# The loads of q, k and v issued from GpSimd instead of SyncE, in a retention layer followed by two feed-forward blocks

## The chip, the cores and the metric

One core of a Trainium2 chip. The metric is the time of one execution on the device in microseconds (us). The engines are TensorE (PE in the profile; its weight loads are PEld), VectorE (DVE), ScalarE (ACT), GpSimd (POOL) and SyncE (SP), which here does nothing but issue transfers. Transfers run on 16 DMA engines, which all issuers share.

## The reference

Three layers run one after the other. The first is a linear attention with decay: for each of 4 batches and 8 heads a 64x64 state is decayed and updated with each of 768 tokens.

```
state = gamma * state + outer(k[t], v[t])
y[t]  = scale * q[t] @ state                  # B=4, H=8, S=768, D=64
```

Its 3072 x 512 result goes through a gated block and then through a block with a sigmoid gate:

```
x = ((x @ w1) * (x @ w2)) @ w3 @ w_out        # 512 -> 1024 -> 1024 -> 512
h = x @ w_in                                  # 512 -> 2048
out = (h * sigmoid(1.702 * h)) @ w_out2       # 2048 -> 512
```

The weights are handed over as 64-bit numbers, and the kernel converts them itself.

## The kernel before

The attention is done in 24 chunks of 128 tokens, six for each batch, in chunked form: scores of a chunk (k by q), a causal mask with decay, outputs from the masked scores and from the state, and an update of the state. All q, k and v values of one chunk are packed into one array of 128 partitions x 2048 floats, 1 MB, so that one transfer fetches them; only the first chunk is fetched in two halves. `Attention.load(c)` (line 203) does that, into one of four buffers named `qkv`. What comes out of a chunk is scaled into `xb` (L291) and stored to device memory (`xd`, L295), except for the first four chunks, which stay on the chip.

The order of the work is written out by hand and is the program order of every engine's queue. `Attention.run` goes over the chunks: in iteration c come the scores of chunk c+1 (L223), the mask (L235), the state update (L249, copied to `state` by ScalarE in L263), `load(c + 3)`, and the outputs of chunk c (L270 from the masked scores, L280 from the state; the first chunk of a batch has no L280). The load of chunk c+3 takes the buffer of chunk c-1, whose last reader is the outputs of chunk c-1.

Between these parts `fill` puts steps of the weight conversion. One weight tile is two halves of 512 columns and ten steps, most of them on VectorE (L112, L104, L121, L125, L133), with ScalarE in L95 and L99. Raw weights come in transfers of 0.5 MB (`fetch`, L85) into five buffers named `raw`; a buffer is free again when L133 has read it, and the next fetch is issued at that point of the program. Every transfer goes through SyncE's queue, in program order: a fetch that waits for VectorE holds whatever stands behind it.

When enough weights are converted, `fill` also multiplies `w3` by `w_out` on TensorE (`psw`, L162 to L164), two half products for each chunk; this is called the mixing here. Then follow the gated block and the last block in tiles of 512 tokens, in which TensorE has matmuls without a break. All of their products are made of three matmuls of split numbers (`mm3`, L162 to L164).

Ahead of the loop the kernel issues, in this order, the load of chunk 0, the mask, the decay factors `dv`, two fetches, the loads of chunks 1 and 2 with factors between them, and three more fetches; two memsets on GpSimd (L336) clear the state.

Of the kernel before, what the change touches and what calls it, by code (L numbers as in the profile page):

```python
# [37 lines left out]
def tile_kernel(  # L38
# [13 lines left out]
    nc = tc.nc  # L52
# [133 lines left out]
    class Attention:  # L186
# [16 lines left out]
        def load(self, c):  # L203
            t = self.tile("qkv", 2048, 4)
            for h in ((0, 1024), (1024, 2048)) if c == 0 else ((0, 2048),):
                nc.sync.dma_start(t[:, slice(*h)], qkv[c][:, slice(*h)])
            qkt[c] = t[:, :1024].rearrange("p (a n t) -> p a n t", a=2, n=NP)
            kvt[c] = t[:, 1024:].rearrange("p (a h d) -> p a h d", a=2, h=H)

# [405 lines left out]
```

## Time and profile before

| | us |
|---|---|
| median of 3 runs | 1090.16 (1087.97 to 1090.22) |
| the profiled execution | 1093.12 |
| its span, from the first instruction to the last | 1091.3 |
| TensorE busy in it | 1056.6 |
| VectorE busy | 485.2 |
| ScalarE busy | 320.6 |
| GpSimd busy | 1.2 |
| bytes moved by the DMA engines | 94.80 MB |

All durations of the trace come from one execution, so sums are made against its 1093.12 us, 1.8 us of which lie around the span. Busy times of engines overlap and don't add up to the span. An issue of a transfer is short on the queue that issues it; the transfer itself goes on for microseconds after.

### The profile page before, as it was taken

The page shows a single profiled execution, that of the slowest core. Times are in us where ns is not written, and L with a number is a line of the kernel's source. Part 1 is how long each engine was busy: PE and PEld are TensorE (multiplying, and loading weights), DVE is VectorE, ACT ScalarE, POOL GpSimd, SP SyncE. Part 2 cuts the span into 40 slices and gives each one's busy share as a digit, 9 for nine tenths or more (in the row PEclk, how much of TensorE's full clock was granted, in tenths as well). Part 3 has the DMA queues.
Part 4 walks back from the last instruction along what each step waited for, and adds up shares of the span by engine and source line. Part 5 has one row for each costly group of instructions (what it writes and reads, how often), then busy time and mean ns, then how long its engine had stood idle before and what let it go on. Part 6 is the DMA issues. An engine that isn't in the chain of part 4 may idle for free.

```text
span 1091.3 us, 13274 instructions
## 1 busy us (share of the span) xinstructions
PE 1056.6 (97%) x5472; PEld 878.1 (80%) x5472; DVE 485.2 (44%) x824; ACT 320.6 (29%) x554; POOL 1.2 (0%) x6
## 2 busy tenths in 40 slices
PE   5779999999999999999999999999999999999998
PEld 4668887888888888888888888888888888888887
DVE  4778888841222221565567752232233233223222
ACT  2233334431212211333344432222222222223222
POOL 0000000000000000000000000000000000000000
PEclk9789999999999999999999999999999999999999
DMA  9888855511010100433323201001001001001001
GB/s 350 288 298 274 290 184 183 182 53 55 10 59 20 58 14 6 135 97 127 105 75 119 77 20 59 1 20 59 1 19 58 1 20 58 1 11 49 1 1 39
DMA packets 38989, 94.80 MB, mean 87 GB/s; under 512 B 3600, under 2 KB 13968, under 8 KB 35984
## 3 DMA queue, kind: packets, MB, share of 16 engines
q1 hardware_dynamic: 38928, 93.95, 25.4%
q8 instruction: 43, 0.70, 0.3%
q14 instruction: 18, 0.15, 0.0%
HBM read 76.11 MB, written 17.83 MB: 86 GB/s over the span
## 4 chain that ended last, share of the span: by engine, by line
PE 92%; DMA 3%; DVE 3%; ACT 1%; issue 1%; SPq 0%
PE psm L164 16%; PE psm L162 16%; PE psm L163 16%; PE acc L164 12%; PE acc L162 12%; PE acc L163 12%; DMA qkv<-in_qkv_dram 3%; PE s L223 2%; PE psw L164 1%; PE psw L162 1%; PE psw L163 1%; PE y L270 1%; PE y L280 1%; DVE pt L235 1%; PE u L249 1%
## 5 line engine op out<-in xcount | busy, mean ns | idle before, releaser
L164 PE MATMUL psm<-xh,wl 128*128 128x512 f32 x768 | 298.9, 389 | 1.5 <-DVE wl L104 1.5
L162 PE MATMUL psm<-xh,wh 128*128 128x512 f32 x768 | 298.8, 389 | 0.0
L163 PE MATMUL psm<-xl,wh 128*128 128x512 f32 x768 | 298.8, 389 | 0.0
L491 DVE TENSOR_TENSOR tmp<-tmp,psm 128x512 f32<-128x512 f32 x96 | 65.9, 687 | 260.7 <-ACT tmp L490 260.7
L164 PEld LDWEIGHTS psm<-xh,wl 128*128 128x128 f32 x768 | 144.2, 188 | 31.9 <-DVE wl L104 2.0
L163 PEld LDWEIGHTS psm<-xl,wh 128*128 128x128 f32 x768 | 144.2, 188 | 30.0
L162 PEld LDWEIGHTS psm<-xh,wh 128*128 128x128 f32 x768 | 144.1, 188 | 29.6
L164 PE MATMUL acc<-wh,hl 128*128 128x512 f32 x384 | 149.4, 389 | 0.0
L163 PE MATMUL acc<-wl,hh 128*128 128x512 f32 x384 | 149.4, 389 | 0.0
L162 PE MATMUL acc<-wh,hh 128*128 128x512 f32 x384 | 149.4, 389 | 0.0
L411 ACT CAST hh<-tmp 128x512 fp32r<-128x512 f32 x144 | 89.4, 621 | 198.2 <-DVE tmp L430 124.0
L412 DVE TENSOR_TENSOR hl<-tmp,hh 128x512 fp32r<-128x512 f32 x144 | 99.6, 692 | 98.9 <-ACT hh L411 98.9
L490 ACT ACTIVATE tmp<-psm 128x512 f32<-128x512 f32 x96 | 57.3, 597 | 280.4 <-PE psm L164 279.5
L430 DVE TENSOR_TENSOR tmp<-tmp,psm 128x512 f32<-128x512 f32 x48 | 33.0, 688 | 184.3 <-PE psm L164 177.0
L162 PEld LDWEIGHTS acc<-wh,hh 128*128 128x128 f32 x384 | 72.1, 188 | 15.0
L164 PEld LDWEIGHTS acc<-wh,hl 128*128 128x128 f32 x384 | 72.0, 188 | 15.1
L163 PEld LDWEIGHTS acc<-wl,hh 128*128 128x128 f32 x384 | 72.1, 188 | 14.9
L162 PE MATMUL acc<-hh,wh 128*128 128x512 f32 x192 | 74.7, 389 | 0.0
L163 PE MATMUL acc<-hl,wh 128*128 128x512 f32 x192 | 74.7, 389 | 0.0
L164 PE MATMUL acc<-hh,wl 128*128 128x512 f32 x192 | 74.7, 389 | 0.0
L99 ACT CAST wh<-x 128x512 fp32r<-128x512 f32 x72 | 44.2, 622 | 80.2 <-DVE x L133 72.9
L429 ACT COPY tmp<-psm 128x512 f32<-128x512 f32 x48 | 28.1, 585 | 114.9 <-PE psm L164 103.2
(44 smaller groups left out, 843.4 us busy)
## 6 DMA issues: line engine op xcount, KB each, us to landing
qkv<-in_qkv_dram SPq DMA_DIRECT2D x23, 1024.0 KB, 8.7
raw<-in_w_dram SPq DMA_DIRECT2D x32, 512.0 KB, 4.7
raw<-in_wo_dram SPq DMA_DIRECT2D x24, 512.0 KB, 4.2
raw<-in_wi_dram SPq DMA_DIRECT2D x16, 512.0 KB, 4.3
yd<-st SPq DMA_DIRECT2D x24, 256.0 KB, 2.7
xr<-yd SPq DMA_DIRECT2D x24, 256.0 KB, 3.2
out_dram<-st SPq DMA_DIRECT2D x24, 256.0 KB, 2.0
xd<-xb SPq DMA_DIRECT2D x20, 256.0 KB, 5.9
```

The source lines that it names most:

```text
L99: nc.scalar.copy(parts[i][0][:, n * WC : (n + 1) * WC], wx[i][n])
L162: nc.tensor.matmul(ps, wh, xh, start=start, stop=False, skip_group_check=True)
L163: nc.tensor.matmul(ps, wh, xl, start=False, stop=False, skip_group_check=True)
L164: nc.tensor.matmul(ps, wl, xh, start=False, stop=stop, skip_group_check=True)
L223: nc.tensor.matmul(sc[c][j][:, p, :], qkt[c][r, 1, p, :], qkt[c][r, 0, p, :], start=True, stop=True,)
L235: nc.vector.tensor_tensor(pt[c][:, j], sc[c][j], self.mask.to_broadcast([P, NP, P]), ALU.mult)
L411: nc.scalar.copy(hi, t)
L412: nc.vector.tensor_tensor(lo, t, hi.bitcast(F32), ALU.subtract)
L429: nc.scalar.copy(t, pa)
L430: nc.vector.tensor_tensor(t, t, pb, ALU.mult)
L490: nc.scalar.activation(t, ps, AF.Sigmoid, scale=ALPHA)
L491: nc.vector.tensor_tensor(t, t, ps, ALU.mult)
```

## The change

In `Attention.load` the 25 transfers of the packed q, k, v chunks are issued from GpSimd's queue. All other transfers stay with SyncE, and the place of the call in the program stays what it was.

```diff
         def load(self, c):
             t = self.tile("qkv", 2048, 4)
             for h in ((0, 1024), (1024, 2048)) if c == 0 else ((0, 2048),):
-                nc.sync.dma_start(t[:, slice(*h)], qkv[c][:, slice(*h)])
+                nc.gpsimd.dma_start(t[:, slice(*h)], qkv[c][:, slice(*h)])
             qkt[c] = t[:, :1024].rearrange("p (a n t) -> p a n t", a=2, n=NP)
             kvt[c] = t[:, 1024:].rearrange("p (a h d) -> p a h d", a=2, h=H)
```

## Rows read from the trace of the kernel before

**Rows 1.** Page, part 1: busy us, share of the span, instructions.

```profile
PE 1056.6 (97%) x5472; PEld 878.1 (80%) x5472; DVE 485.2 (44%) x824; ACT 320.6 (29%) x554; POOL 1.2 (0%) x6
```

**Rows 2.** Stages: start:end, us, busy us of each engine, PEclk, DMA share, GB/s.

```profile
0.00:12.88 12.88, 2.08 (x16) 1.78 (x16) 1.90 (x4) 2.60 (x3) 1.19 (x6) 1.00 0.86 320
...
92.40:167.00 74.60, 73.25 (x677) 60.73 (x676) 63.12 (x118) 26.61 (x51) 0.00 (x0) 1.00 0.72 252
167.00:1091.00 924.00, 919.04 (x4054) 760.52 (x4052) 358.59 (x594) 266.70 (x451) 0.00 (x0) 1.00 0.16 52
...
12.88:92.40 79.52, 62.23 (x729) 55.11 (x730) 61.58 (x111) 24.67 (x50) 0.00 (x0) 0.81 0.84 299
...
60.00:80.00 20.00, 12.64 (x150) 11.18 (x146) 13.77 (x26) 6.02 (x12) 0.00 (x0) 0.80 0.92 312
```

**Rows 3.** Chain that ended last, 40 to 93 us: start, us, what.

```profile
41.13 8.63 DMA qkv<-in_qkv_dram
...
56.79 9.33 DMA qkv<-in_qkv_dram
...
70.71 8.91 DMA qkv<-in_qkv_dram
```

**Rows 4.** VectorE groups, 41.13 to 92.40 us, idle last; TensorE's waits, 12.88 to 92.40.

```profile
L235 DVE TENSOR_TENSOR pt<-s,mask 128x512 f32<-128x512 f32 x17 | 10.9, 683 | 2.7 <-PE s L223 2.7
L216 DVE TENSOR_TENSOR vs<-qkv,dv 128x512 f32<-128x512 f32 x9 | 6.2, 686 | 5.5 <-DMA qkv<-in_qkv_dram 5.5
L291 DVE TENSOR_TENSOR xb<-y,dy 128x512 f32<-128x512 f32 x9 | 6.2, 686 | 5.1 <-PE y L280 4.8 <-PE y L270 0.3
...
PE s L223 <- DMA qkv<-in_qkv_dram: 23.8, 6, 6.5
```

**Rows 5.** Timeline of TensorE: start, us, what, [idle before, releaser].

```profile
12.89 2.08 PE L223 MATMUL s<-qkv 64*128 64x128 f32 x16 [6.49 <-DMA qkv<-in_qkv_dram]
...
30.97 1.16 PE L280 MATMUL y<-qkv,state 128*128 128x128 f32 x8
...
44.12 1.16 PE L280 MATMUL y<-qkv,state 128*128 128x128 f32 x8
...
52.81 1.92 PE L270 MATMUL y<-pt,vs 128*64 128x128 f32 x16
...
61.11 1.16 PE L280 MATMUL y<-qkv,state 128*128 128x128 f32 x8
...
79.75 2.08 PE L223 MATMUL s<-qkv 64*128 64x128 f32 x16 [3.38 <-DMA qkv<-in_qkv_dram]
...
85.68 1.21 PE L223 MATMUL s<-qkv 64*128 64x128 f32 x16
```

**Rows 6.** SyncE's waits, 12.88 to 92.40 us: total, times, longest.

```profile
SPq L85 <- DVE x L133: 41.5, 9, 10.0
```

**Rows 7.** DMA issues, 12.88 to 92.40 us: count, KB each, median us to landing.

```profile
qkv<-in_qkv_dram SPq DMA_DIRECT2D x13, 1024.0 KB, 8.9
raw<-in_w_dram SPq DMA_DIRECT2D x7, 512.0 KB, 5.7
```

**Rows 8.** Timeline of all engines at the start.

```profile
0.73 0.98 POOL L336 MEMSET state<- 128x512 f32 x2 [0.29 <-POOLq L598]
...
12.87 0.69 DVE L216 TENSOR_TENSOR vs<-qkv,dv 128x512 f32<-128x512 f32 x1 [4.80 <-DMA qkv<-in_qkv_dram]
...
16.12 0.76 ACT L263 COPY state<-u 64x256 f32<-64x256 f32 x2 [5.77 <-PE u L249]
```

**Rows 9.** VectorE groups, 12.88 to 92.40 us: busy us, mean ns of one, idle.

```profile
L133 DVE SCALAR_TENSOR_TENSOR x<-raw,x 128x512 int32<-128x512 int32 x10 | 6.8, 683 | 0.0
...
L112 DVE TENSOR_SCALAR x<-x 128x512 f32<-128x512 f32 x12 | 5.0, 418 | 0.0
L121 DVE TENSOR_SCALAR x<-x 128x512 int32<-128x512 int32 x11 | 4.6, 417 | 0.0
```

## The prediction

> **What bounds the kernel now.** I read the busy times first. TensorE is busy 1056.6 of 1091.3 us [rows 1], so whatever the change does must come out of the 35 us in which TensorE has nothing to do, or be added to them. Then the stages [rows 2]: from 167 us to the end TensorE is busy 919.04 of 924.00 us and from 92.40 to 167 us 73.25 of 74.60. Those two stages run at TensorE's pace; a transfer that lands earlier there ends nothing earlier. The stage that isn't at TensorE's pace is the attention loop before the weight products set in, from the second chunk's scores at 12.88 us to 92.40 us: 79.52 us, in which TensorE has 62.23 us of work (at a mean granted clock of 0.81, so that part of it even at the lower level, 1.2 GHz), VectorE 61.58 us, and the DMA engines a share of 0.84. Nothing is full there, so I asked for the chain: in its second half the chain jumps three times onto a load of q, k, v, for 8.63, 9.33 and 8.91 us [rows 3]. These are the loads of chunks 7, 10 and 12. The waits say what that costs the engines: between 41.13 and 92.40 us VectorE idles 5.5 us for a load itself, 2.7 us for the scores that the late load held back, and 5.1 us for the outputs behind them, 13.3 us together; over the whole stage TensorE waits 23.8 us in 6 places for a load [rows 4].
>
> Why are the loads late? A load of chunk c+3 goes into the buffer that chunk c-1 leaves, so it may start when the outputs of chunk c-1 have been computed. For chunk 7 that is at 30.97 + 1.16 = 32.13 us [rows 5], yet SyncE issues it at 41.13 us, where its piece of the chain begins [rows 3]: 9.0 us late. For chunk 12 it is 61.11 + 1.16 = 62.27 us against 70.71 us: 8.4 us late. For chunk 10 it is 52.81 + 1.92 = 54.73 us against 56.79 us: 2.1 us. The reason stands in SyncE's waits: its fetches of raw weights (L85) wait for VectorE's L133 41.5 us in 9 places of the stage, 10.0 us the longest [rows 6], and in program order those fetches stand ahead of the load. The load pays for a wait that isn't its own.
>
> **The change part by part.** *The issue moves.* 25 issues leave SyncE's queue. GpSimd has 6 short instructions in the whole kernel, all before 12.88 us (1.19 us busy, [rows 2]), so from then on nothing stands ahead of a load on its queue but the loads before it, and each waits for its own buffer alone. So the head-of-line delay goes: 9.0 us for chunk 7, 8.4 us for chunk 12, 2.1 us for chunk 10. I price the landing at the stage's median from issue to landing, 8.9 us [rows 7], plus 1 us for an issue that is made by GpSimd (bounds below). Chunk 7 would then land at 32.1 + 9.9 = 42 us, before its scores are wanted (behind the outputs of chunk 5, at 44.12 + 1.16 = 45.3 us, [rows 5]): stall gone. Chunk 12 lands at 72.2 us; its scores ran at 79.75 us, after a wait of 3.4 us [rows 5]: gone. Chunk 10 lands at 64.6 us rather than 66.2: only 1.6 us less.
>
> *What is late next.* Two floors stand under the stage. VectorE's: 79.52 - 13.3 = 66.2 us. The DMA engines': the stage's bytes are the same, share 0.84 of 79.52 us, which is 66.8 us at a share of 1.00, and 72.6 us at 0.92, the share of 60 to 80 us [rows 2], a stretch that holds loads, fetches and stores as the others do. I take 0.92, as I saw no such stretch of 20 us fuller, so the stage loses 79.52 - 72.6 = 6.9 us; at 1.00 it would lose 12.7.
>
> *What the new issue costs.* No row shows GpSimd issuing a DMA. From below: an issue can't cost less than nothing beside SyncE's, which already lies mostly in waits, though a load with a ring of its own may land sooner than 8.9 us since the 0.5 MB raw fetches (5.7 us to landing, [rows 7]) no longer stand ahead of it; the fastest that I allow is that 5.7 us. From above: the nearest row of work that GpSimd does is a pair of memsets, 0.98 us [rows 8]; and if GpSimd could work only while VectorE is idle (VectorE is busy 77% of the stage), that 0.98 would stretch by 1/0.23, to 4.3 us. I take 1 us, the undisturbed row, because a load is two or three simple address lists, and keep 0 to 4.3 for the range. The first four loads and the two memsets of the state also stand in one line on GpSimd now: the memsets started at 0.73 us, and at 1 us per load would start near 5 us; the state is wanted at 16.12 us, when the first update is copied into it [rows 8]. That part costs nothing, unless each of the four holds GpSimd for over 3.8 us.
>
> *The start.* By 12.88 us the chip had moved 12.88 x 320 GB/s = 4.1 MB [rows 2], and the second load landed then; its scores are the chain. With two queues the order of those bytes changes. VectorE idled till 12.87 us anyway [rows 8], so chunk 0 has room; chunk 1 has none. If the loads get two thirds of the bandwidth, their 2.1 MB and half as much beside them, 3.1 MB, take 9.8 us, some 2 us less than now counting 1 us for the slower issue; if the halves are equal, 4.2 MB take 13.1 us, and with the issue it is 1 to 3 us more than now. Range -2 to +3, taken +1.
>
> *What SyncE gains.* 25 issues of some 0.4 us and its own waits for buffers. SyncE's fetches then go out when VectorE frees a raw buffer, as before: they wait for VectorE, not for the loads, so I price this at nothing. The cover is the five raw buffers: a load and a fetch now share the engines, so a fetch lands later by up to its own 5.7 us, and five buffers are three to six iterations of slack. Were that gone, ScalarE's L95 and the whole VectorE order behind it would wait.
>
> *After 92.40 us.* The order of instructions is fixed, so TensorE's 73.25 + 919 us move forward as they are. DMA share there is 0.72, and the loads of chunks 17 to 23 lie under TensorE's work.
>
> Sum: -6.9 + 1 = -5.9 us. The profiled execution took 1093.12 us (span 1091.3), so 1087.2 by its own time; the median of the three runs is 2.96 us below that execution, which puts the forecast at 1084.3 us.
>
> **A rule against it.** The rows say that the loads wait for SyncE's order and that SyncE's own issue time is small: 25 issues are about 10 us, on a queue with long waits. The Trainium skill, "DMA: Bandwidth & Descriptors", section "Issuing engines are not separate DMA queues", says that DMAs of all issuers end on the same 16 engines and interleave, and that issuing from several saves no more than the sequencer's issue time. By that rule nothing is gained: rival 1. The trace agrees that the engines are shared (0.92 at the fullest), but 41.5 us of waits ahead of the loads are not issue time.
>
> **The rivals.**
> 1. *Same bytes, same engines.* The loads start earlier and land when they did, since what they gain in order they lose in sharing with fetches and stores: an earlier load only pushes the next fetch. For it: shares of 0.84 to 0.92. Against it: the share is a mean, and it falls where SyncE is held (a load was possible at 32.13 us and came at 41.13). The stage stays at 79.5, the start costs -2 to +3: 1088 to 1092, say 1090.5.
> 2. *The issue on GpSimd is slow, and the loop runs at its latency.* The scores of chunk c+3 come two iterations after the outputs of chunk c-1, so two iterations can't be shorter than the time L from a free buffer to a landed load. From 12.89 to 85.68 us there are 12 iterations [rows 5], 6.07 us each: the change loses from L = 12.1 us on. With 8.9 us for the transfer that leaves 3.2 us for GpSimd. At the upper bound, 4.3 us, L is 13.2 and an iteration 6.6 us: 12 x 0.53 = 6.4 us more, and with the start's +3 the forecast would be 1099.6. For it: VectorE, busy 77% of the stage, also issues 23 TENSOR_SCALARs there at 418 ns against 683 ns for its other operations of the same size [rows 9], so it runs in a faster mode in 9.6 us of the 79.5; if GpSimd were held only then, 1 us would become 1.1. Against it: the upper bound needs GpSimd held by every VectorE instruction. The Trainium skill, "SBUF — State Buffer", section "SBUF: two separate sides", says that GpSimd can't write descriptors while VectorE runs an operation in a mode that takes both ports, and gives 620 ns that became 3100. By that figure, an estimate, a load gains 2.5 us and the change stays just on the good side of 3.2. No run here shows it yet.
> 3. *The latency is all that counted, and the engines have room.* Then VectorE's floor holds, limited by a share of 1.00: -12.7, and 1077.5.
>
> **How the numbers follow.** About 0.2% (2.2 us) is what a measurement of this kernel can tell from no change. Forecast (a gain of 2.5 to 10 us): 0.48. Rival 3: 0.10. Rival 1: 0.18. Rival 2: 0.24. Faster is the first two together, 0.58; same 0.18; slower 0.24. The likeliest is the forecast, 1084.3 us, by itself 1080 to 1088. Both signs have weight, so the range goes further: down to rival 3 with half a microsecond, 1077, and up to half of rival 2's cases, 1096.
>
> **What would show it.** Right: the chain from 40 to 92 us without loads of 8 to 9 us; TensorE's waits for loads down from 23.8 us to some 10; the DMA share of the stage at 0.9 or above; the weight products of the mixing stage set in near 86 us rather than 92.4; the stages behind it as long as now. Wrong: GpSimd's issues of 3 us or more each, loads landing over 12 us after their buffer came free, iterations over 6.1 us (rival 2); a share still at 0.84 with loads in flight for 14 us or more (rival 1). If fetches land so late that ScalarE's L95 waits more than a few microseconds, the cover that I priced at nothing is gone.

## The result, and the profile after

| | before | after |
|---|---|---|
| median of the runs, us | 1090.19 (1087.97 to 1091.27, 4 runs) | 1080.56 (1079.61 to 1083.18, 4 runs) |
| the profiled execution, us | 1093.12 | 1081.2 |
| its span, us | 1091.3 | 1079.1 |

The ratio is 0.9914, with a 95% interval of 0.9899 to 0.9929: 9.4 us faster (7.7 to 11.0). The forecast was 1084.3 us, within 1077 to 1096. A second comparison of the same two kernels, further down, gave 0.9923 (0.9909 to 0.9937).

Where the time went can be read from the stages. These are the stages of the kernel after, cut at the same two places of the program as [rows 2]: the second chunk's scores and the first product of the mixing (start:end, length, busy us of PE, PEld, DVE, ACT, POOL, granted clock, DMA share, GB/s).

```profile
0.00:13.28 13.28, 2.08 (x16) 1.79 (x16) 1.90 (x4) 2.61 (x3) 3.88 (x11) 1.00 0.83 292
13.28:80.23 66.95, 57.21 (x729) 49.54 (x730) 60.88 (x111) 24.61 (x49) 7.08 (x13) 0.95 0.95 365
80.23:154.80 74.57, 73.22 (x677) 60.75 (x676) 63.15 (x118) 27.26 (x51) 3.73 (x7) 1.00 0.72 245
154.80:1079.00 924.20, 919.02 (x4054) 760.67 (x4052) 358.73 (x594) 266.79 (x451) 0.00 (x0) 1.00 0.16 52
```

The start takes 13.28 us instead of 12.88, the attention stage 66.95 instead of 79.52, the mixing 74.57 instead of 74.60, the rest 924.20 instead of 924.00. So all of it lies in the attention stage, and it arrives at the end undiminished. VectorE is now busy 91% of that stage, and the DMA engines' share is 0.95.

Inside the stage, first the waits for loads (TensorE's, then VectorE's groups with their idle time last), which answer to [rows 4], here all over the whole stage:

```profile
PE s L223 <- DMA qkv<-in_qkv_dram: 6.9, 5, 4.2
...
L235 DVE TENSOR_TENSOR pt<-s,mask 128x512 f32<-128x512 f32 x27 | 17.4, 688 | 1.1 <-PE s L223 1.1
L216 DVE TENSOR_TENSOR vs<-qkv,dv 128x512 f32<-128x512 f32 x14 | 9.7, 690 | 1.5 <-DMA qkv<-in_qkv_dram 1.5
L291 DVE TENSOR_TENSOR xb<-y,dy 128x512 f32<-128x512 f32 x13 | 9.0, 690 | 2.2 <-PE y L280 1.2 <-DMA dy<-in_cy_dram 0.5 <-PE y L270 0.5
```

TensorE waited 23.8 us for loads and now waits 6.9, of which 4.2 us are the first one.

Then GpSimd's timeline of the loads of chunks 7, 10 and 12, and TensorE's rows that free their buffers and use them (start, length, what, idle time before with its releaser):

```profile
32.10 0.53 POOL L206 DMA_DIRECT2D qkv<-in_qkv_dram  x1 [5.39 <-PE y L280]
46.62 0.53 POOL L206 DMA_DIRECT2D qkv<-in_qkv_dram  x1 [1.74 <-DVE xb L291]
57.39 0.53 POOL L206 DMA_DIRECT2D qkv<-in_qkv_dram  x1 [4.01 <-PE y L280]
...
30.64 1.16 PE L280 MATMUL y<-qkv,state 128*128 128x128 f32 x8
43.99 1.71 PE L223 MATMUL s<-qkv 64*128 64x128 f32 x16
45.63 0.69 PE L249 MATMUL u<-vs,qkv 128*64 128x64 f32 x16
55.93 1.16 PE L280 MATMUL y<-qkv,state 128*128 128x128 f32 x8
68.97 1.16 PE L223 MATMUL s<-qkv 64*128 64x128 f32 x16
```

The buffer of chunk 7 comes free at 30.64 + 1.16 = 31.80 us and the load is issued at 32.10; that of chunk 12 at 57.09, issued at 57.39. The buffer of chunk 10 is the one that chunk 6 leaves, the first chunk of a batch: its outputs (L270) don't read it, so its last reader is the update L249, which ends at 45.63 + 0.69 = 46.32 us, and the load is issued at 46.62. The 9.0 and 8.4 us of [rows 3, 5] have become 0.3. The scores of chunks 7 and 12, at 43.99 and 68.97 us, wait for no load.

SyncE still waits for VectorE about as long as it did in [rows 6]; the times to landing answer to [rows 7]:

```profile
SPq L85 <- DVE x L133: 45.2, 9, 15.9
...
qkv<-in_qkv_dram POOLq DMA_DIRECT2D x13, 1024.0 KB, 8.3
raw<-in_w_dram SPq DMA_DIRECT2D x7, 512.0 KB, 8.1
```

The 41.5 us of waiting have become 45.2, but now no load stands behind them, only fetches, factors and stores. A load lands in 8.3 us instead of 8.9, and a fetch pays for it with 8.1 instead of 5.7.

### The profile page after: what moved, and what is told of

It reads as the page before. It is cut to its first block, busy times and chain, and to the rows that moved or that the text cites. A ratio compares the mean times of both kernels' runs of the same rounds, so it can differ in the third digit from the quotient of the medians.

```text
span 1079.1 us, 13290 instructions
## 1 busy us (share of the span) xinstructions
PE 1051.5 (97%) x5472; PEld 872.7 (81%) x5472; DVE 484.7 (45%) x824; ACT 321.3 (30%) x554; POOL 14.7 (1%) x31
## 4 chain that ended last, share of the span: by engine, by line
PE 91%; DMA 3%; issue 2%; DVE 2%; ACT 1%; SPq 0%; POOL 0%; POOLq 0%; DVEq 0%
PE psm L164 16%; PE psm L162 16%; PE psm L163 16%; PE acc L164 12%; PE acc L162 12%; PE acc L163 12%; DMA dy<-in_cy_dram 2%; PE psw L164 1%; PE psw L162 1%; PE psw L163 1%; PE y L280 1%; PE s L223 1%; DVE pt L235 1%; DMA qkv<-in_qkv_dram 1%; PE y L270 1%
```

## The experiments

All medians are of several runs beside runs of the kernel before on the same chip; the ratio is to those.

| | median us | ratio (95%) | mixing begins, us |
|---|---|---|---|
| before (in the profile) | 1090.2 | 1 | 92.16 |
| changed | 1080.56 | 0.9914 (0.9899 to 0.9929) | 79.99 |
| e1: fetches on GpSimd, not loads | 1088.46 | 0.9977 (0.9968 to 0.9986) | 85.36 |
| e2: loads and fetches on GpSimd | 1092.84 | 1.0016 (1.0005 to 1.0027) | 91.22 |
| e3: SyncE alone, load called earlier | 1084.38 | 0.9943 (0.9929 to 0.9958) | 82.58 |
| e4: changed, loads 2.4 us later | 1085.97 | 0.9954 (0.9940 to 0.9968) | 84.79 |
| e5: changed, loads 4.8 us later | 1095.28 | 1.0038 (1.0024 to 1.0051) | 93.88 |
| e6: first chunk from SyncE | 1082.40 | 0.9921 (0.9908 to 0.9934) | 80.24 |
| e7: changed, no clamp | 1079.09 | 0.9889 (0.9871 to 0.9908) | 79.72 |
| e9: chunks 0 to 3 from SyncE | 1086.04 | 0.9956 (0.9941 to 0.9972) | 84.51 |
| e10: changed again | 1081.56 | 0.9923 (0.9909 to 0.9937) | 78.71 |
| e11: start in order | 1082.23 | 0.9930 (0.9914 to 0.9945) | 81.05 |
| e12: changed, half the fetched bytes | 1080.06 | 0.9911 (0.9895 to 0.9927) | 78.97 |
| e13: fetches of the loop on GpSimd | 1085.82 | 0.9959 (0.9944 to 0.9974) | 85.26 |

In the two profiles of before and after, what lies behind the first product of the mixing takes the same 999.1 us (1091.3 - 92.16 and 1079.1 - 79.99). So the last column tells where a kernel gained or lost ahead of it. It is of one execution each, and the medians decide.

**Is it the order, the engine, or a second queue?** The change moves three things at once: a load no longer stands behind fetches, its transfer is made by another issuer, and it has a queue of its own. Four runs take these apart.

*e2* puts the fetches on GpSimd too, so that issuer and queue are changed but the order is that of before.

```diff
-        nc.sync.dma_start(raw, src.rearrange("p (c w) -> p c w", w=2))
+        nc.gpsimd.dma_start(raw, src.rearrange("p (c w) -> p c w", w=2))
```

> Loads and fetches both on GpSimd, in the program order of the kernel before, so a load again stands behind the fetches; stores and factors on SyncE. Theory A (order): the gain goes, 1087 to 1091 us, and the loads of chunks 7 and 12 are again issued 8 us after their buffer came free. Theory B (GpSimd's transfers themselves are faster): the gain stays or grows, 1078 to 1082. Theory C (what counts is that loads and stores are on two queues and share the engines packet by packet): the gain stays, 1080 to 1083.

The gain is gone: 1092.84 us, 0.16% slower than before. Its timelines (GpSimd, then TensorE) show the old picture on the new queue:

```profile
41.94 0.53 POOL L85 DMA_DIRECT2D raw<-in_wo_dram  x1 [9.40 <-DVE x L133]
43.73 0.53 POOL L85 DMA_DIRECT2D raw<-in_w_dram  x1 [1.27 <-issue]
44.25 1.04 POOL L206 DMA_DIRECT2D qkv<-in_qkv_dram  x2
...
34.22 1.16 PE L280 MATMUL y<-qkv,state 128*128 128x128 f32 x8
52.72 2.08 PE L223 MATMUL s<-qkv 64*128 64x128 f32 x16 [6.88 <-DMA qkv<-in_qkv_dram]
```

Chunk 7's buffer is free at 35.38 us; GpSimd waits 9.4 us for VectorE's L133 on behalf of a fetch, and the load goes out at 44.25, 8.9 us late. The scores wait 6.88 us. The second scores come at 15.43 us, 2.5 later than before, which is more than the 1.8 us by which e2's median is the slower one; so even if all of that start reaches the end, some 0.7 us of gain hide behind it. Neither the issuer nor a queue apart from the stores brings the 9.4: theories B and C fall.

*e3* leaves everything with SyncE and moves only the call.

```diff
                 if c + 1 < NC:
                     self.scores(c + 1)
+                if c + 3 < NC:
+                    self.load(c + 3)
                 fill(c, 0)
...
-                if c + 3 < NC:
-                    self.load(c + 3)
                 fill(c, 2)
```

> All transfers on SyncE as before; only the call of the load of chunk c+3 is moved in the program from behind the state update to right behind the scores of chunk c+1, ahead of that iteration's first two weight steps. Theory A (order): loads that had fetches of their own iteration ahead of them, as those of chunks 7 and 12 (9.0 and 8.4 us late), are issued some 8 us earlier, while that of chunk 10 (2.1 us late) stays; so half to three quarters of the gain without any second queue, 1082 to 1086 us. Theories B and C (the issuing engine, or two queues): nothing, 1088 to 1091.

1084.38 us: two thirds of the gain (0.57% of 0.86%) with no second queue at all. In SyncE's timeline chunk 7's load, whose buffer is free at 31.71 us, is issued on time, while chunk 10's, free at 43.78 + 0.69 = 44.47 us when chunk 6's update L249 ends, still stands behind two fetches and a store and goes out at 50.68; its scores wait.

```profile
31.74 0.33 SPq L206 DMA_DIRECT2D qkv<-in_qkv_dram  x1
...
49.97 0.62 SPq L85 DMA_DIRECT2D raw<-in_w_dram  x1
50.68 0.56 SPq L206 DMA_DIRECT2D qkv<-in_qkv_dram  x1
...
60.09 1.43 PE L223 MATMUL s<-qkv 64*128 64x128 f32 x16 [3.46 <-DMA qkv<-in_qkv_dram]
```

*e1* moves the other side: the edit of e2, made in the kernel before, with the loads left on SyncE.

> The other side of the queue is moved: the loads of q, k, v stay with SyncE and the fetches of raw weights (L85) are issued from GpSimd. Theory A (order: a load was held behind fetches that wait for VectorE): the fetches wait on a queue of their own, the loads have only the stores of xb ahead of them, so most of the gain of the change comes here too: 1080 to 1084 us against 1090, and the stage before the mixing takes 67 to 71 us rather than 79.5. Theory B (a load issued by GpSimd moves in less DMA time per byte, and that is the gain): the loads are as before, so 1088 to 1091.

A miss: 1088.46 us, only 2.6 less than before, where 1080 to 1084 were expected. Part of it is the start: the first five fetches go out from GpSimd at once and share the engines with chunk 1's load, so the second scores come at 15.84 us instead of 12.89. *e13* gives that back: it is e1, but the five fetches ahead of the loop stay with SyncE.

```diff
-        nc.sync.dma_start(raw, src.rearrange("p (c w) -> p c w", w=2))
+        q = nc.sync if n < R_BUFS else nc.gpsimd
+        q.dma_start(raw, src.rearrange("p (c w) -> p c w", w=2))
```

> As e1 (fetches on GpSimd, loads on SyncE), but the five fetches ahead of the loop stay with SyncE, so that the start is that of the kernel before. In e1 the second chunk's scores came at 15.84 us instead of 12.89, and the stage behind them took 69.5 us. Theory A (order) with that start given back: scores of chunk 1 at 12.5 to 13.2 us, the mixing from 82 to 84 us, 1082 to 1086 us. If e1's shortfall had another cause (loads on SyncE's ring land later than loads on GpSimd's), it stays at 1087 to 1089.

1085.82 us, 4.1 less than before and inside what order foretold, at its upper end; the mixing begins later than the 82 to 84 us expected. What is still missing against the changed kernel stands in its timelines (SyncE, then TensorE):

```profile
43.09 0.60 SPq L296 DMA_DIRECT2D xd<-xb  x1
43.80 0.55 SPq L207 DMA_DIRECT2D qkv<-in_qkv_dram  x1
...
37.65 1.16 PE L281 MATMUL y<-qkv,state 128*128 128x128 f32 x8
```

(Lines are one later in this kernel.) Chunk 8's buffer is free at 38.81 us, but its load stands behind the store of `xb`, which waits for VectorE until 43.09: 5.0 us late. The loads had two kinds of transfers ahead of them that wait for VectorE, fetches and stores. The prediction saw only the fetches. The change takes the loads from behind both, e13 from behind the fetches alone, e3 from behind some of either.

**Does the loop run at the load's latency?** The prediction's second rival gave a price: two iterations can't be shorter than the time L from a free buffer to a landed load. e4 and e5 put four and eight memsets of the buffer itself between the two, from chunk 4 on.

```diff
             t = self.tile("qkv", 2048, 4)
+            for _ in range(4 if c > 3 else 0):          # 8 in e5
+                nc.gpsimd.memset(t[:, :512], 0.0)
```

> The changed kernel with four memsets on GpSimd, of 512 columns of the buffer itself, between a free buffer and its load, for chunks 4 and on: some 2 us more from free buffer to landed load. Theory L (two iterations can't be shorter than that latency): it goes from about 8.6 to 10.7 us, so an iteration from 4.9 to 5.0 to 5.4 us, and the twelve iterations ahead of the mixing take 1 to 6 us more: 1082 to 1087 us, most likely 1084. Theory D (VectorE or the bytes hold the stage, and the latency has room): within 1 us of the changed kernel.

> The same with eight memsets, some 4 us more: the latency is then about 12.8 us, beyond the 12.1 us at which the prediction put the break-even with the kernel before (a little less if the transfers land sooner in a slower loop). Theory L: an iteration of 5.8 to 6.4 us, 1089 to 1098 us, so about the time of the kernel before or slower. Theory D: 1081 to 1085.

1085.97 and 1095.28 us: both inside what the latency foretold, and the second slower than the kernel before. L is first put together from its parts: the memsets (2.43 and 4.77 us in the timelines), 0.3 us to the issue, and the median to landing (8.3 and 7.0 us). Beside it stands what the traces have, the mean over chunks 4 to 13 of the time from the last read of the buffer to the landed load. The iterations are counted from chunk 3's scores to chunk 13's.

| | L by its parts, us | L in the trace, us | half of that | an iteration, us |
|---|---|---|---|---|
| changed | 0.3 + 8.3 = 8.6 | 8.7 | 4.3 | (72.18 - 21.44) / 10 = 5.07 |
| e4 | 2.43 + 0.3 + 8.3 = 11.0 | 10.9 | 5.4 | (76.00 - 21.22) / 10 = 5.48 |
| e5 | 4.77 + 0.3 + 7.0 = 12.1 | 13.5 | 6.8 | (87.05 - 22.23) / 10 = 6.48 |
| before | | 12.7 | 6.3 | (85.68 - 23.13) / 10 = 6.26 |

The changed kernel lies above half of L, so something else holds it. e4 lies on it, and so does the kernel before, whose late issues are part of its L. e5 was meant to sit at the break-even of 12.1 us and lies beyond it, since a chunk's memsets stand in line behind those of the chunk before (TensorE's last read of chunk 6's buffer, then GpSimd's memsets and loads of chunks 9 and 10, in e5):

```profile
47.73 0.69 PE L251 MATMUL u<-vs,qkv 128*64 128x64 f32 x16
...
48.99 4.79 POOL L206 MEMSET qkv<- 128x512 f32 x8
54.07 0.53 POOL L208 DMA_DIRECT2D qkv<-in_qkv_dram  x1 [0.30 <-DVE xb L293]
54.59 5.08 POOL L206 MEMSET qkv<- 128x512 f32 x8
59.97 0.53 POOL L208 DMA_DIRECT2D qkv<-in_qkv_dram  x1 [0.30 <-POOL qkv L206]
```

Chunk 10's buffer is free at 48.42 us, its memsets begin at 54.59, and its load goes out at 59.97, 11.55 us late. So the break-even lies between e4 (L 10.9 us, 0.46% faster than before) and e5 (13.5 us, 0.38% slower); a straight line between the two puts it at 12.3 us, an estimate, beside the prediction's 12.1.

**What holds the changed kernel now?** In the stage VectorE is busy 91% and the DMA share is 0.95. e7 takes VectorE's clamp out, e12 halves the bytes of the later fetches.

```diff
             for x in wx[i]:
-                nc.vector.tensor_scalar(x, x, LEAST, MOST, ALU.max, ALU.min)
                 yield i - 1
```

> The changed kernel without the clamp of the weights' magnitudes (L112, one VectorE operation in five of the conversion; this part of the computation is left out). In the stage ahead of the mixing there are 12 of them, at 0.34 us of VectorE's time each, 4.1 us. Theory V (VectorE is now what holds the stage, busy 60.88 of 66.95 us): 3 to 4 us less than the changed kernel, 1077 to 1078.5. Theory B (the DMA engines hold it, share 0.95): 0 to 1.5 us less.

```diff
-        raw = big.tile([P, WC, 2], I32, tag="r", bufs=R_BUFS, name="raw")
-        nc.sync.dma_start(raw, src.rearrange("p (c w) -> p c w", w=2))
+        k = 0
+        if n < R_BUFS:
+            slots.append(big.tile([P, WC, 2], I32, tag=f"r{n}", bufs=1, name="raw"))
+        else:
+            k = WC // 2
+        raw = slots[n % R_BUFS]
+        nc.sync.dma_start(raw[:, k:], src.rearrange("p (c w) -> p c w", w=2)[:, k:])
```

> The changed kernel with half the bytes in every fetch of raw weights from the sixth on (the first half of each buffer keeps what it held, so that part of the weights is wrong): 2.5 MB less of the stage's 24.4 MB, with VectorE's work as it is. Theory B (the DMA engines hold the stage, share 0.95): the stage goes from 67 us to its VectorE floor, some 62 to 64 us, 3 to 5 us less than the changed kernel. Theory V (VectorE holds it): 0 to 1 us less.

> The changed kernel itself, beside the next two on the same chip, so that differences of 2 us can be told. It should give 0.990 to 0.993 of the kernel before, 1080 to 1083 us.

The stretch from 13.3 to 80 us of e10 (the changed kernel again), e7 and e12, in this order:

```profile
13.30:80.00 66.70, 56.75 (x734) 48.91 (x735) 61.78 (x113) 24.52 (x49) 7.60 (x14) 0.97 0.99 372
...
13.30:80.00 66.70, 55.54 (x729) 48.43 (x730) 57.94 (x100) 24.52 (x49) 6.89 (x13) 0.95 0.97 365
...
13.30:80.00 66.70, 58.73 (x733) 51.22 (x734) 61.77 (x113) 24.54 (x49) 7.57 (x14) 0.92 0.93 338
```

Without the clamp VectorE has 3.8 us less to do in it. The single profile shows no gain from that: the stretch holds no more of TensorE's work than in e10, and the mixing begins at 79.72 us against 78.71. The medians do: a ratio of 0.9889 against 0.9914 and 0.9923 of the changed kernel, 2.7 and 3.7 us, with an interval that overlaps the first one's and ends just below the second's (0.9908 against 0.9909). That is near what theory V asked for. With fewer bytes the DMA share falls to 0.93, and the median is 1.5 us below e10, measured beside it, with intervals that overlap, where theory B asked for 3 to 5. So VectorE is the likelier of the two to hold the stage; how much each would give is not settled by these runs.

**Can the start be had back?** The change moved the first scores from 4.32 to 7.01 us and the second from 12.89 to 13.29 [rows 5]. Three versions tried to mend that. e6 issues the two halves of chunk 0 from SyncE:

```diff
-                nc.gpsimd.dma_start(t[:, slice(*h)], qkv[c][:, slice(*h)])
+                q = nc.sync if c == 0 else nc.gpsimd
+                q.dma_start(t[:, slice(*h)], qkv[c][:, slice(*h)])
```

> The changed kernel, but the two halves of the first chunk's load are issued from SyncE, ahead of everything else, as in the kernel before; all other loads from GpSimd. The change put the first scores from 4.32 to 7.01 us and the second from 12.89 to 13.29. Theory S (the start is given away, since GpSimd's first loads share the engines with the fetches): first scores at 4 to 5 us, the second chunk's at 9 to 12, and 1 to 4 us less than the changed kernel, 1077 to 1080 us. Theory T (the stage is held by VectorE and by the bytes, whatever comes first): within 0.5 us of the changed kernel, 1080 to 1081.

1082.40 us, 0.9921: no better than the changed kernel. The first scores come at 4.36 us, but the small factors `dv`, now behind chunk 0, land so late that VectorE begins at 12.23 us instead of 9.92.

e9 puts chunks 0 to 3 on SyncE, with `dv` ahead and chunk 1 ahead of the first fetches:

```diff
-                nc.gpsimd.dma_start(t[:, slice(*h)], qkv[c][:, slice(*h)])
+                q = nc.sync if c < 4 else nc.gpsimd
+                q.dma_start(t[:, slice(*h)], qkv[c][:, slice(*h)])
...
+            nc.sync.dma_start(attention.dv, cv)
             attention.load(0)
             nc.sync.dma_start(attention.mask, cmask)
-            nc.sync.dma_start(attention.dv, cv)
+            attention.load(1)
             fetch(0)
             fetch(1)
             attention.factors(0)
-            attention.load(1)
-            attention.factors(1)
             attention.load(2)
+            attention.factors(1)
```

> The changed kernel with another start: the loads of chunks 0 to 3 on SyncE's queue, with the small factors dv ahead and chunk 1 ahead of the first two fetches; loads of chunks 4 and on from GpSimd. With one queue the order holds: chunk 0 should land near 5 us, chunk 1 near 8 (2.2 MB at 400 GB/s), the first two fetches near 10 to 11. Theory S (the start is on the path): the second chunk's scores at 8 to 9 us instead of 13.3, VectorE sets in earlier, and 1 to 4 us of it reach the end, 1077 to 1080 us. Theory B (the bytes of the whole stage hold it, and they don't change): within 1 us of the changed kernel.

A miss, 1086.04 us: by the ratios some 4 us slower than the changed kernel. The second scores did come at 9.76 us, but chunk 3's load, on SyncE behind five fetches and three factors, shows what the change is about once more (SyncE's waits up to 14 us, then its and TensorE's timeline):

```profile
SPq L207 <- DMA raw<-in_wo_dram: 1.0, 1, 1.0
...
12.35 0.33 SPq L207 DMA_DIRECT2D qkv<-in_qkv_dram  x1
...
28.17 2.08 PE L224 MATMUL s<-qkv 64*128 64x128 f32 x16 [7.14 <-DMA qkv<-in_qkv_dram]
```

Its buffer was free from the start, yet it goes out 8 us later than in the changed kernel, where GpSimd issued it at 4.40 us: SyncE held it until a raw fetch ahead of it had landed. It lands 15.7 us after its issue, as long as in the changed kernel (20.05 - 4.40), so it is late by its issue. GpSimd's load of chunk 4, issued at 13.22 us, went past it and landed at 23.00, against 28.04.

e11 leaves chunks 0 and 1 with SyncE, `dv` and chunk 1 ahead as in e9, and holds GpSimd's first load until chunk 0 has landed:

```diff
-                nc.gpsimd.dma_start(t[:, slice(*h)], qkv[c][:, slice(*h)])
+                q = nc.sync if c < 2 else nc.gpsimd
+                q.dma_start(t[:, slice(*h)], qkv[c][:, slice(*h)])
...
             for s in attention.state:
                 nc.gpsimd.memset(s, 0.0)
+            gate0 = p0.tile([P, 1], F32, name="gate0")
+            nc.gpsimd.tensor_copy(gate0, kvt[0][:, 1, H - 1, D - 1 :])
+            attention.load(2)
```

> The changed kernel with a start in order: dv, the two halves of chunk 0, the mask and chunk 1 from SyncE ahead of the first fetches, and GpSimd's first load (chunk 2) held until the last element of chunk 0 has landed, by a copy of that element; chunks 2 and on from GpSimd. Theory S (the start is on the path, and the earlier trial lost because chunk 3's load stood behind fetches): chunk 1's scores at 9 to 11 us instead of 13.3, no load of 15 us, and 1 to 3 us less than the changed kernel. Theory B (the DMA engines, at a share of 0.95 over the stage, hold it, and the bytes stay): within 1 us of the changed kernel.

1082.23 us, 0.7 above e10: within 1 us, as theory B said. The second scores come at 9.61 us, 4 us earlier, and the lead is gone ten microseconds later: VectorE's L112 waits for ScalarE's L95, which waits for raw weights that the loads have pushed back, and the vs of chunk 2 starts at 20.15 us in e11 (first fence line below: the wait; second: that vs), against 20.21 in the changed kernel (third).

```profile
15.29 0.43 DVE L112 TENSOR_SCALAR x<-x 128x512 f32<-128x512 f32 x1 [2.12 <-ACT x L95]
20.15 0.68 DVE L217 TENSOR_TENSOR vs<-qkv,dv 128x512 f32<-128x512 f32 x1
...
20.21 0.69 DVE L216 TENSOR_TENSOR vs<-qkv,dv 128x512 f32<-128x512 f32 x1
```

From 10 to 20 us the DMA engines are full in both (share 1.02, 419 and 420 GB/s). What is put ahead there puts something else back. No version beat the changed kernel.

## Why the prediction was right, point by point

*The cause* was right and is shown: loads stood in SyncE's queue behind transfers that wait for VectorE. The delays of 9.0 and 8.4 us became 0.3 us, e2 brought them back with the gain undone, and e3 had two thirds of the gain without a second queue. But the cause was told too narrowly: the prediction named the fetches (41.5 us of waits) and not the stores of `xb`. SyncE's waits before stand in the stores' lines too (20.2 us in L295 over the stage), and e13 shows what these cost a load (5.0 us for chunk 8).

*The stage* was forecast 6.9 us shorter and became 12.57 us shorter in the profile. The term that was mis-sized is the floor of the DMA engines: the prediction capped the share at 0.92, the fullest stretch of 20 us that it saw, and so put the stage at 72.6 us. The share reached 0.95 in the profile and 0.99 in that of e10, the same kernel; from 10 to 20 us it stood at 1.02 in the kernel before as well. Nor is the engines' time fixed by the bytes: 0.95 of 66.95 us is 63.6 us, against 66.8 before, for as many bytes or more (365 GB/s over 66.95 us, 299 over 79.52). So the cap didn't bind, and the stage came to 66.95 us, near the 66.2 of VectorE's floor. In the profile the stage behaved as the third rival said (-12.7); in the medians the whole gain is 9.4 us, between that and the forecast's 5.9, so the forecast was 3.7 us too slow. Of the 11.9 us between the two profiled executions, some 2.3 are which execution was profiled: that of before lay 2.9 us above its median, that of after 0.6.

*Chunk 10* was forecast to keep most of its stall, as its load was read to be 2.1 us late. That reading, like the account of the kernel ahead of it, took the outputs of a chunk for the last reader of its buffer; for chunk 6, the first of a batch, it is the update ahead of them, in the kernel before:

```profile
51.91 1.12 PE L249 MATMUL u<-vs,qkv 128*64 128x64 f32 x16
```

The buffer was free at 51.91 + 1.12 = 53.03 us, so the load, at 56.79, was 3.8 us late. In the changed kernel it is 0.3, and the scores wait for nothing.

*The issue on GpSimd* was priced at 1 us with a range to 4.3; an issue takes 0.53 us in most rows above, and the load lands in 8.3 us rather than 8.9, so L is 8.6 us, not 9.9. The rule of the Trainium skill, "SBUF — State Buffer", section "SBUF: two separate sides", that GpSimd can't write descriptors under VectorE's two-port operations, shows in one issue of the stage at most. It is chunk 4's, made while two TENSOR_SCALARs ran one behind the other; in e7, which has only one of them there, the same issue takes 0.53 us (GpSimd and VectorE in the changed kernel, then GpSimd in e7):

```profile
16.73 0.75 POOL L206 DMA_DIRECT2D qkv<-in_qkv_dram  x1 [11.81 <-DVE pt L235]
16.61 0.42 DVE L112 TENSOR_SCALAR x<-x 128x512 f32<-128x512 f32 x1
16.94 0.42 DVE L121 TENSOR_SCALAR x<-x 128x512 int32<-128x512 int32 x1
...
16.89 0.53 POOL L205 DMA_DIRECT2D qkv<-in_qkv_dram  x1 [11.95 <-DVE pt L234]
```

That is 0.2 us, far from the 620 ns that became 3100. VectorE is busy 91% of the stage, but only 9.8 us of it are TENSOR_SCALARs, of 0.42 us each, so the rule was hardly put to the test.

*The start* was priced at +1 us and cost 0.4 (13.29 against 12.89).

*What SyncE gains* was priced at nothing with five raw buffers as the cover. The cover held, narrowly: a fetch lands in 8.1 us rather than 5.7, and ScalarE's L95 waits 4.8 us for raw weights in the stage, which is the prediction's own sign of a cover that is gone; but VectorE's L112 shows no idle time in it.

*Rival 1*, that bytes and engines make any order equal, fell: e2 and the changed kernel move the same bytes. The rule that the prediction set against the change, of the Trainium skill, "DMA: Bandwidth & Descriptors", section "Issuing engines are not separate DMA queues", is half borne out: another issuer by itself brought nothing (e2, 1.0016), but it saves more than issue time when it takes a transfer from behind somebody else's wait. *Rival 2* had the right mechanism and price, as e4 and e5 show; its latency stayed 3.5 us short of the point from which it decides (8.6 against 12.1 us).

## What to carry to other kernels

A queue that issues transfers in program order hands the wait of one transfer to all that stand behind it; look at what each issue queue waits for, and at how late a transfer goes out after the last read of its buffer, before counting bytes. Moving it to an idle queue, or calling it earlier, gives that back; moving it together with what blocked it gives nothing. Where a load takes the buffer left two iterations ahead of its use, the loop can't run faster than half the latency from a free buffer to a landed load (5.48 us beside 5.4 in e4), so that latency, and not the issue time, is what a slower issuer may spend.

## What the runs showed of the hardware

The delaying memsets of e4 had a side effect: they made VectorE's TENSOR_SCALARs slower and its other operations not. VectorE's groups from 13.3 to 80 us in the changed kernel, then in e4 (busy us, mean ns):

```profile
L133 DVE SCALAR_TENSOR_TENSOR x<-raw,x 128x512 int32<-128x512 int32 x10 | 6.9, 688 | 0.0
L112 DVE TENSOR_SCALAR x<-x 128x512 f32<-128x512 f32 x12 | 5.1, 423 | 0.0
L121 DVE TENSOR_SCALAR x<-x 128x512 int32<-128x512 int32 x11 | 4.7, 423 | 0.0
...
L133 DVE SCALAR_TENSOR_TENSOR x<-raw,x 128x512 int32<-128x512 int32 x10 | 6.8, 679 | 0.0
L121 DVE TENSOR_SCALAR x<-x 128x512 int32<-128x512 int32 x10 | 6.1, 608 | 0.0
L112 DVE TENSOR_SCALAR x<-x 128x512 f32<-128x512 f32 x12 | 5.8, 487 | 0.0
```

Beside GpSimd's memsets they take 487 and 608 ns instead of 423, in e5 575 and 584. GpSimd's issues of transfers alone left them at 423, against 418 in [rows 9]. That a fast mode of VectorE and GpSimd exclude each other is what the Trainium skill says in "SBUF — State Buffer", section "Who interferes with whom"; here the memsets agree, and of the issues only a few: chunk 4's 0.75 us above, and 0.89 us for the same load in e9, again over two TENSOR_SCALARs.

TensorE's own work shrank with the waits: 62.23 us busy in the stage before [rows 2], 57.21 after, for the same 729 matmuls, with the granted clock at a mean of 0.95 instead of 0.81. A share of the matmuls that ran at the lower level, 1.2 GHz, after a wait for a load now runs at 2.4: chunk 12's scores took 2.08 us behind their wait [rows 5] and take 1.16 without it. The prediction gave that no term of its own, and what it is worth apart from the waits isn't shown.
